# Constant matmuls in the waits of TensorE, a third weight tile split during the first gather, one more job of weight prefetch, and more ticks per step of later routing

## The chip, the cores and the metric

One core of a Trainium2 chip runs the whole program as one launch. The metric is device microseconds of one execution; the number compared is the median of several executions.

## The reference

Three stages in a row, all float32:

```
attn:  4 batches x 8 heads, 512 local + 32 global queries, head size 64
       local: |i-j| <= 32 window plus the 32 global keys; global: all 544 keys
x = attn output as [2304 tokens, 512]
moe:   logits = x @ w_gate                       # 8 experts
       for (token, e) by falling logit: take it if the token is free and e has < 288 tokens
       h = relu(x[mask] @ w1[e]); out[mask] = h @ w2[e]        # 512 -> 1024 -> 512
moe2:  out = (silu(x @ w_gate2) * (x @ w_val)) @ w_out         # 512 -> 1536 -> 512
```

The greedy assignment fills one expert after another: each routing phase finds which expert fills next and which 288 tokens it gets.

## The kernel before

**Stages.** `attention` runs 40 units (n = 0 to 39, plus 3 to drain) of scores, softmax, transposes and products. Between them it runs steps of `Convert`, which loads the second layer's float64 weights as pairs of words (`cv_raw`, 512 KB each), takes a magnitude on ACT (L116), builds float32 words on DVE (L122 to L124) into `cv_f` and stores them to a scratch `wd` (L128). A job is loaded `LD` jobs ahead of its magnitude, in `RAWB` buffers of `cv_raw`; `cv_f` has `FB` = 4 buffers. All these loads and stores, those of q, k and v, and the stores of x go through SP's queue, in program order.

**The expert stage.** Tokens are handled as 4 groups of 2 experts. For each expert, `moe(k, e)` runs blocks h(0) to h(7) and y(0) to y(5), then y(6) and y(7) together; each block is 12 matmuls of 272 columns (a product is three: high by high, high by low, low by high). `group` then runs the second layer of both: 12 x 2 blocks of 24 such matmuls, and an output stage with 512-column matmuls. Weights come as tiles of 512 KB: a load into one of 4 `raw` buffers on SP's queue, a rounding copy on ACT (L979) and a residual on DVE (L980, "split") into one of 6 `wHL` buffers. `pump` splits the tile that is needed and at most one ahead of it, if that was asked for at least `LAG` = 4 ticks ago; `load` keeps up to 3 loads outstanding. An expert's tiles in order: w1 0, w1 1, w2 0, w1 2, w2 1, w1 3, w2 2, w2 3; h(0), h(1) use the first, h(2), h(3) the second, y(0), y(1) the third.

**Routing in the background.** `background` is a generator that walks the routing phases 0 to 7: `after(k-1)`, then `phase(k)`: `best`, six search steps (a compare L678 on DVE, 17 small matmuls L685, four small DVE operations from L688), the expert's number `eis` (from which the weight loads take their address), the ranks, and the token list `idx` (17 matmuls L743). Every block of `moe` and `group` ends with `tick()`, which resumes the generator if the number of ticks of its last yield is over. `hurry` sets those numbers: for phase 1, a yield of 1 costs none and a larger one 2 ticks; for later phases a yield of more than 1 costs one tick more as long as the conversion isn't finished (`s.cv.finished`). A moe has 14 ticks, a group's 24 blocks 48, its output stage 12.

**Fetching an expert's rows.** When a phase is done, `fetch(k)` issues three indirect gathers on POOL's queue (L880), yields how many routing ticks to let pass (`GW` = 6 for expert 1, `GL` = 12 later, counted in the yields' own numbers), then transposes three blocks on PE (L898), with a copy on ACT (xH, L900) and a residual on DVE (xL, L901) for each. `wait_for(k)`, at the start of `moe(k)`, resumes the generator again and again until x of expert k is there; then the blocks go into three PSUM banks without yields between them (`s.waiting`), else all through one bank.

**Order.** The program order of every engine is the order in which this code emits it; engines run their queues in order and wait on semaphores. For expert 0, before the change, `fetch` splits two weight tiles, and x(0) is transposed at the third routing yield after the gather.

Of the kernel before, what the change touches and what calls it, by code (L numbers as in the profile page):

```python
# [14 lines left out]
ALU = mybir.AluOpType  # L15
# [49 lines left out]
CV0, CV1 = 3, 6  # L65
QB = 8
PL = 2
RAWB, CB, FB, LD = 5, 3, 4, 3
NC = 30
EN = 36  # L70
UO, LW = 0, 39
# [470 lines left out]
class Router:  # L542
# [110 lines left out]
    def phase(s, n):  # L653
        nc, V, K, b = s.nc, s.nc.vector, s.K, s.bank
        last = n == E - 1
        if n:
            yield from s.best(n)
            yield TB, 0.0
        if not last:
            lo = s.gmin  # L660
            KS, NR = KN[0]
            cmp, ge = s.cmp[:, :, 0:KS], s.ge[:, 0:KS]
            V.tensor_scalar(s.d, s.hi, s.gmin, 1e-26, op0=ALU.subtract, op1=ALU.max)
            Td = s.Td[:, 0:KS * NR].rearrange("p (r k) -> p r k", k=KS)
            V.tensor_scalar(Td, s.io[0], s.d, None, op0=ALU.mult)
            def step(k):

                return Td[:, k, 1:2]
            def bound(k):

                V.tensor_scalar(s.m1, k1, KS - 1.5, 1e38, op0=ALU.is_ge, op1=ALU.mult)
                V.tensor_scalar(s.k2, k1, 1.0, None, op0=ALU.add)
                V.scalar_tensor_tensor(s.cd, s.k2, step(k), old, op0=ALU.mult, op1=ALU.add)
                V.scalar_tensor_tensor(s.hi, s.cd, s.m1, s.hi, op0=ALU.max, op1=ALU.min)
            parts = ((0, 9), (9, NCH)) if n == 0 else ((0, NCH),)
            for k in range(NR):
                for c0, c1 in parts:
                    V.scalar_tensor_tensor(cmp[:, c0:c1], Td[:, k, None, :].to_broadcast([128, c1 - c0, KS]), lo,  # L678
                                           s.v[:, c0:c1, None].to_broadcast([128, c1 - c0, KS]), op0=ALU.add, op1=ALU.is_le)
                if k:  # L680
                    bound(k - 1)
                yield TA, RF
                cnt = b[:, 0:KS]
                for c in range(NCH):
                    nc.tensor.matmul(cnt, s.ohr[:, c].rearrange("p r e -> p (r e)"), cmp[:, c, :], start=c == 0, stop=c == NCH - 1)  # L685

                k1, new = s.k1[k % 2], s.lo2[k % 2]
                V.tensor_scalar(ge, cnt, s.nd, -1.0, op0=ALU.is_ge, op1=ALU.add, accum_out=s.ke)  # L688
                V.tensor_reduce(k1, s.ke.to_broadcast([128, 32]), axis=AX.X, op=ALU.max, apply_transpose=True)
                V.scalar_tensor_tensor(new, k1, step(k), lo, op0=ALU.mult, op1=ALU.add)  # L690
                old, lo = lo, new

            V.scalar_tensor_tensor(s.ew, s.ke, k1, s.w8p, op0=ALU.is_ge, op1=ALU.mult)
            V.tensor_reduce(s.em, s.ew.to_broadcast([128, 32]), axis=AX.X, op=ALU.max, apply_transpose=True)
            bound(NR - 1)
            V.tensor_scalar(s.G, s.v, lo, None, op0=ALU.is_ge)
            V.tensor_scalar(s.A, s.v, s.hi, None, op0=ALU.is_ge)
            V.tensor_tensor(s.G, s.G, s.A, op=ALU.subtract)
        else:
            V.scalar_tensor_tensor(s.e8, s.pen, OUTV / 2, s.w8, op0=ALU.is_ge, op1=ALU.mult)  # L700
            V.tensor_reduce(s.em, s.e8, axis=AX.X, op=ALU.max)
            V.tensor_scalar(s.A, s.v, OUTV / 2, None, op0=ALU.is_ge)
            V.memset(s.G, 0.0)
        V.tensor_scalar(s.eis[n], s.em, -1.0, 8.0, op0=ALU.mult, op1=ALU.add)
        s.known = n
        yield 1, 0.0

        Mb = s.Mb.rearrange("p (u c) -> p u c", u=2)
        V.scalar_tensor_tensor(Mb[:, 0], s.v0, s.em, s.A, op0=ALU.is_equal, op1=ALU.mult)
        V.scalar_tensor_tensor(Mb[:, 1], s.v0, s.em, s.G, op0=ALU.is_equal, op1=ALU.mult)  # L710
        if n:
            V.scalar_tensor_tensor(Mb[:, 0], s.ac, s.em, Mb[:, 0], op0=ALU.is_equal, op1=ALU.add)

        V.tensor_tensor_scan(s.Pc[:, 1:1 + 2 * NCH], s.ones, s.Mb, 0.0, op0=ALU.mult, op1=ALU.add)
        yield 2, RP if n == 0 else 0.7
        p = b[:, 320:354]
        nc.tensor.matmul(p, s.tri, s.Mb, start=True, stop=False)
        nc.tensor.matmul(p, s.onesb, s.Pc[:, 0:2 * NCH], start=False, stop=True)

        V.scalar_tensor_tensor(s.M.rearrange("p u c -> p (u c)"), p, 1.0, s.Mb, op0=ALU.add, op1=ALU.mult)  # L720
        V.scalar_tensor_tensor(s.pp, s.M[:, 0], -1.0, s.M[:, 1], op0=ALU.add, op1=ALU.add)
        W = nc.gpsimd if n == 0 else V
        V.tensor_scalar(s.lo, s.pp, 127, None, op0=ALU.bitwise_and)
        if n == 0:
            V.tensor_copy(s.lob[:, 0:NCH], s.lo)
        V.tensor_tensor(s.hb, s.pp[:, None, :].to_broadcast([128, 4, NCH]), s.thr[:, :, None].to_broadcast([128, 4, NCH]), op=ALU.is_ge)
        yield 1, 0.0
        W.tensor_tensor(s.h3, s.hb[:, 0:3], s.hb[:, 1:4], op=ALU.subtract)
        W.tensor_tensor(s.rh, s.h3.rearrange("p k c -> p c k")[:, :, :, None].to_broadcast([128, NCH, 3, 2]),
                        s.rid[:, :, None, :].to_broadcast([128, NCH, 3, 2]), op=ALU.mult)  # L730
        for c0, c1 in ((0, 8), (8, NCH + 1)):
            yield 1, 0.0
            if n == 0:
                V.tensor_tensor(s.ol[:, :, c0:c1], s.iota2[:, :, c0:c1], s.lob[:, None, c0:c1].to_broadcast([128, 128, c1 - c0]), op=ALU.is_equal)
            else:

                x = slice(c0, min(c1, NCH))
                N = x.stop - c0
                V.tensor_tensor(s.olc[:, x], s.iota[:, None, :].to_broadcast([128, N, 128]), s.lo[:, x, None].to_broadcast([128, N, 128]), op=ALU.is_equal)
        yield TQ, 0.0  # L740
        q = b[:, 384:390]
        for c in range(NCH):
            nc.tensor.matmul(q, s.olc[:, c] if n else s.ol[:, :, c], s.rh[:, c].rearrange("p k u -> p (k u)"), start=c == 0, stop=c == NCH - 1)  # L743
        q3 = q.rearrange("p (k u) -> p k u", u=2)
        V.tensor_copy(s.idxf[n], q3[:, :, 1])
        V.scalar_tensor_tensor(s.idx[n], q3[:, :, 0], 16.0, s.idxf[n], op0=ALU.mult, op1=ALU.add)
        V.tensor_copy(s.idxf[n], s.idx[n])
# [24 lines left out]
TE = CAP  # L772
OT = 4
GW, GL = 6, 12
CV2 = 0.4
LA0 = 3
MO = 1
# [3 lines left out]
class Ffn:  # L781
# [37 lines left out]
    def background(s):  # L819
# [3 lines left out]
        for k in range(E):  # L823
            for y in s.steps(k):
                yield s.hurry(k, y)
                if pend and now is None and s.moes >= pend[0] - 1:
                    now = s.fetch(pend.pop(0))
                    left = next(now)
                    yield 1, 0.0
                elif now is not None:  # L830
                    left -= y[0]
                    if left <= 0:
                        x = next(now)
                        if isinstance(x, int):
                            left = x
                        else:
                            yield x
                            yield from now
                            now = None
            if k < E:  # L840
                s.done_phase = k
            pend.append(k)
            if now is None and s.moes >= pend[0] - 1:
                now = s.fetch(pend.pop(0))
                left = next(now)
                yield 1, 0.0
# [21 lines left out]
    def hurry(s, k, y):  # L868

        if k == 1:  # L870
            return (0 if y[0] == 1 else TA, y[1])

        return (y[0] + (y[0] > 1 and k > 1 and not s.cv.finished), y[1])

    def fetch(s, k):

# [4 lines left out]
                                         in_offset=bass.IndirectOffsetOnAxis(ap=s.R.idx[k][0:n, blk:blk + 1], axis=0))  # L881
        if k == 0:

            yield 2
            for m in range(2):
                s.pump(m, 0)
                yield 1
        else:
            yield GW if k == 1 else GL
        xH = s.pool.tile([128, 4, TE], F32R, name="xH", bufs=2)  # L890
        xL = s.pool.tile([128, 4, TE], F32R, name="xL", bufs=2)
        s.xT[k] = (xH, xL)
        for blk, n in enumerate((128, 128, 16)):
# [7 lines left out]
            nc.vector.tensor_tensor(xL[:, :, sl], p, xH[:, :, sl].bitcast(F32), op=ALU.subtract)  # L901
            yield 0, 0.0
            if not s.waiting:
                yield 1, 0.0
        s.ready.add(k)

    def convert(s, n):
# [105 lines left out]
    def wait_for(s, k):  # L1013
        s.waiting = True
        while k not in s.ready:
            next(s.bgen)
            s.load()
        s.waiting = False

    def moe(s, k, e):  # L1020
# [132 lines left out]
    def run(s, ext):  # L1153
# [3 lines left out]
        for _ in s.bgen:  # L1157
            if s.R.known == 0:
                while s.nd < LA0:
                    s.dma(s.nd); s.asked[s.nd] = -1; s.nd += 1  # L1160
            if s.done_phase == 0:
                break
        s.wait_for(0)
# [55 lines left out]
```

## Time and profile before

| | us |
|---|---|
| median of 3 executions | 929.43 (929.22 to 931.23) |
| profiled execution, its own time | 931.21 |
| its span, first to last instruction | 929.4 |
| PE busy in the span | 852.3 (92%) |
| DVE busy | 595.3 (64%) |
| ACT busy | 393.8 (42%) |
| POOL busy | 110.5 (12%) |
| mean granted TensorE clock | 0.96 of full speed |

PE is TensorE, PEld its weight loads, DVE VectorE, ACT ScalarE, POOL GpSimd, SP SyncE (here a DMA queue, SPq). A line such as L980 is a line of the kernel. In a timeline row, "x12" merges twelve instructions, and the bracket at the end gives how long the engine was idle before and what released it. PEclk is the granted TensorE clock as a share of 2.4 GHz: 1.00 is that level and 0.50 is 1.2 GHz.

### The profile page before, as it was taken

The page shows a single profiled execution, that of the slowest core. Times are in us where ns is not written, and L with a number is a line of the kernel's source. Part 1 is how long each engine was busy: PE and PEld are TensorE (multiplying, and loading weights), DVE is VectorE, ACT ScalarE, POOL GpSimd, SP SyncE. Part 2 cuts the span into 40 slices and gives each one's busy share as a digit, 9 for nine tenths or more (in the row PEclk, how much of TensorE's full clock was granted, in tenths as well). Part 3 has the DMA queues.
Part 4 walks back from the last instruction along what each step waited for, and adds up shares of the span by engine and source line. Part 5 has one row for each costly group of instructions (what it writes and reads, how often), then busy time and mean ns, then how long its engine had stood idle before and what let it go on. Part 6 is the DMA issues. An engine that isn't in the chain of part 4 may idle for free.

```text
span 929.4 us, 19215 instructions
## 1 busy us (share of the span) xinstructions
PE 852.3 (92%) x7567; PEld 787.9 (85%) x7567; DVE 595.3 (64%) x1482; ACT 393.8 (42%) x823; POOL 110.5 (12%) x189
## 2 busy tenths in 40 slices
PE   6999999727779898999999899999999999999997
PEld 5887887516769897979999898899999889999985
DVE  3687786785979887847888876466454335544410
ACT  4797887502235432314443332245344234443300
POOL 5343241020000100101101000210100020000002
PEclk9999999956979899999999999999999999999999
DMA  7898898333337632234542213365322245522101
GB/s 174 219 274 240 259 266 292 118 99 108 112 95 247 198 119 75 76 113 156 182 137 82 103 62 99 114 210 162 131 92 91 91 144 174 159 69 92 46 1 56
DMA packets 109386, 128.62 MB, mean 138 GB/s; under 512 B 57392, under 2 KB 75056, under 8 KB 109296
## 3 DMA queue, kind: packets, MB, share of 16 engines
q1 hardware_dynamic: 105856, 118.35, 41.4%
q0 software_dynamic: 2896, 8.92, 2.7%
q8 instruction: 59, 0.97, 0.4%
q14 instruction: 31, 0.25, 0.1%
q10 hardware_dynamic: 544, 0.13, 0.1%
HBM read 109.02 MB, written 18.35 MB: 137 GB/s over the span
## 4 chain that ended last, share of the span: by engine, by line
PE 52%; issue 21%; DVE 17%; ACT 4%; DMA 3%; SPq 1%; POOL 1%; POOLq 0%; DVEq 0%; ACTq 0%
PE b L1009 9%; PE b L1011 9%; PE b L1010 8%; PE b L1114 4%; PE b L1115 4%; PE b L1116 4%; DVE wHL L980 3%; PE s L303 2%; DVE r_cmp L678 2%; PE tr L323 2%; DMA cv_raw<-moe_w_val 2%; PE o L334 2%; DVE b L1091 1%; ACT dH L1092 1%; PE o L339 1%
## 5 line engine op out<-in xcount | busy, mean ns | idle before, releaser
L1009 PE MATMUL b<-yH,wHL 128*128 128x272 f32 x768 | 226.5, 295 | 0.1
L1011 PE MATMUL b<-yH,wHL 128*128 128x272 f32 x768 | 222.9, 290 | 0.0
L1010 PE MATMUL b<-yL,wHL 128*128 128x272 f32 x768 | 222.3, 290 | 0.0
L980 DVE TENSOR_TENSOR wHL<-raw,wHL 128x1024 fp32r<-128x1024 f32 x136 | 163.7, 1222 | 41.0 <-ACT wHL L979 40.2
L979 ACT CAST wHL<-raw 128x1024 fp32r<-128x1024 f32 x136 | 139.2, 1047 | 77.3 <-PE b L1116 45.7
L1009 PEld LDWEIGHTS b<-yH,wHL 128*128 128x128 f32 x768 | 146.2, 190 | 5.4 <-issue 5.0
L1010 PEld LDWEIGHTS b<-yL,wHL 128*128 128x128 f32 x768 | 146.6, 191 | 0.0
L1011 PEld LDWEIGHTS b<-yH,wHL 128*128 128x128 f32 x768 | 146.2, 190 | 0.0
L1092 ACT CAST dH<-b 128x272 fp32r<-128x272 f32 x96 | 37.1, 387 | 181.9 <-DVE b L1091 178.3
L1011 PE MATMUL b<-xH,wHL 128*128 128x272 f32 x252 | 74.6, 296 | 3.5 <-DVE wHL L980 3.4
L1011 PE MATMUL b<-dH,wHL 128*128 128x272 f32 x256 | 74.7, 292 | 2.3 <-DVE wHL L980 2.3
L1009 PE MATMUL b<-xH,wHL 128*128 128x272 f32 x252 | 75.5, 300 | 1.3 <-ACT wHL L979 0.7
L1009 PE MATMUL b<-dH,wHL 128*128 128x272 f32 x256 | 75.6, 295 | 1.0 <-ACT wHL L979 1.0
L1114 PE MATMUL b<-wHL,dH 128*128 128x512 f32 x192 | 76.4, 398 | 0.0
L1115 PE MATMUL b<-wHL,dL 128*128 128x512 f32 x192 | 75.9, 395 | 0.0
L1116 PE MATMUL b<-wHL,dH 128*128 128x512 f32 x192 | 75.8, 395 | 0.0
L1010 PE MATMUL b<-dL,wHL 128*128 128x272 f32 x256 | 74.3, 290 | 0.6 <-DVE dL L1037 0.6
L1091 DVE TENSOR_TENSOR b<-b,si 128x272 f32<-128x272 f32 x96 | 42.8, 445 | 49.4 <-PE b L1011 49.4
L1010 PE MATMUL b<-xL,wHL 128*128 128x272 f32 x252 | 73.9, 293 | 0.0
L1036 ACT ACTIVATE dH<-b 128x272 fp32r<-128x272 f32 x64 | 25.5, 398 | 106.8 <-PE b L1011 102.6
L1093 DVE TENSOR_TENSOR dL<-b,dH 128x272 fp32r<-128x272 f32 x96 | 42.4, 442 | 43.6 <-ACT dH L1092 43.6
L880 POOL DMA_INDIRECT xg<-xd,r_idx x24 | 25.7, 1072 | 296.7 <-DVE r_ac L754 104.6
(237 smaller groups left out, 1612.8 us busy)
## 6 DMA issues: line engine op xcount, KB each, us to landing
raw<-wd SPq DMA_DIRECT2D x72, 512.0 KB, 3.7
raw<-moe_w SPq DMA_DIRECT2D x64, 512.0 KB, 3.7
wd<-cv_f SPq DMA_DIRECT2D x36, 256.0 KB, 6.2
cv_raw<-moe_w_gate SPq DMA_DIRECT2D x12, 512.0 KB, 6.6
cv_raw<-moe_w_val SPq DMA_DIRECT2D x12, 512.0 KB
cv_raw<-moe_w_out SPq DMA_DIRECT2D x12, 512.0 KB, 5.5
xd<-xt SPq DMA_DIRECT2D x16, 256.0 KB, 3.8
st<-k_l SPq DMA_DIRECT2D x28, 128.0 KB, 5.5
```

Source lines behind the costliest of these rows:

```text
L880: nc.gpsimd.indirect_dma_start(out=xg[0:n, blk, :], out_offset=None, in_=s.K.xd[:, :], in_offset=bass.IndirectOffsetOnAxis(ap=s.R.idx[k][0 ...
L979: nc.scalar.copy(w[:, 0], raw)
L980: nc.vector.tensor_tensor(w[:, 1], raw, w[:, 0].bitcast(F32), op=ALU.subtract)
L1009: nc.tensor.matmul(out, wH, xH, start=start, stop=False)
L1010: nc.tensor.matmul(out, wH, xL, start=False, stop=False)
L1011: nc.tensor.matmul(out, wL, xH, start=False, stop=stop)
L1091: nc.vector.tensor_tensor(b, b, si, op=ALU.mult)
L1092: nc.scalar.copy(dH[:, f, :], b)
L1093: nc.vector.tensor_tensor(dL[:, f, :], b, dH[:, f, :].bitcast(F32), op=ALU.subtract)
L1114: nc.tensor.matmul(ob[i], dh, H[:, f % 2, :], start=f == 0, stop=False)
L1115: nc.tensor.matmul(ob[i], dl, H[:, f % 2, :], start=False, stop=False)
L1116: nc.tensor.matmul(ob[i], dh, L[:, f % 2, :], start=False, stop=f == 11)
```

## The change

Seven edits: (1) `Convert` gets 7 `cv_raw` buffers and loads a job 4 jobs ahead (5 and 3 before). (2) `eis` is computed right after `em`, before the last bound. (3) In phase 0 the operation `h3` goes from POOL to DVE. (4) `fetch(0)` emits 4 constant matmuls (128 x 512, bf16) after the gathers, splits three tiles without `pump`, and emits 6 more before the transposes; later fetches emit 8 before and 14 after their yield, each only if TensorE is then in `wait_for`. (5) A fetch for k > 0 goes on at the next routing yield once `wait_for` runs. (6) `hurry` adds its tick for all of phases 2 to 7, and a fetch yields 2 ticks between blocks. (7) `wait_for(0)` calls no `load()`, and the first three loads count as asked `LAG` ticks earlier.

```diff
-RAWB, CB, FB, LD = 5, 3, 4, 3
+RAWB, CB, FB, LD = 7, 3, 4, 4
...
             V.tensor_reduce(s.em, s.ew.to_broadcast([128, 32]), axis=AX.X, op=ALU.max, apply_transpose=True)
+            V.tensor_scalar(s.eis[n], s.em, -1.0, 8.0, op0=ALU.mult, op1=ALU.add)
             bound(NR - 1)
...
-        V.tensor_scalar(s.eis[n], s.em, -1.0, 8.0, op0=ALU.mult, op1=ALU.add)
+            V.tensor_scalar(s.eis[n], s.em, -1.0, 8.0, op0=ALU.mult, op1=ALU.add)
...
-        W.tensor_tensor(s.h3, s.hb[:, 0:3], s.hb[:, 1:4], op=ALU.subtract)
+        V.tensor_tensor(s.h3, s.hb[:, 0:3], s.hb[:, 1:4], op=ALU.subtract)
...
+W0, W1, W2, W3 = 4, 6, 8, 14
...
-                    if left <= 0:
+                    if left <= 0 or s.waiting and k > 1:
...
-        return (y[0] + (y[0] > 1 and k > 1 and not s.cv.finished), y[1])
+        return (y[0] + (y[0] > 1 and k > 1), y[1])
+
+    def warm(s, n):
+        x = s.R.iota2.rearrange("p w c -> p (w c)")[:, 0:512]
+        for _ in range(n):
+            s.nc.tensor.matmul(s.B[s.hb[1]], s.K.identb, x, start=True, stop=True)
...
         if k == 0:
+            s.warm(W0)
             yield 2
-            for m in range(2):
-                s.pump(m, 0)
+            for m in range(3):
+                s.parts(m); s.np += 1
                 yield 1
+            s.warm(W1)
         else:
+            if s.waiting:
+                s.warm(W2)
             yield GW if k == 1 else GL
+            if s.waiting:
+                s.warm(W3)
...
             if not s.waiting:
-                yield 1, 0.0
+                yield 2, 0.0
...
             next(s.bgen)
-            s.load()
+            if k:
+                s.load()
...
-                    s.dma(s.nd); s.asked[s.nd] = -1; s.nd += 1
+                    s.dma(s.nd); s.asked[s.nd] = -LAG; s.nd += 1
```

## Rows read from the trace of the kernel before

**Rows 1.** Windows by stage of the expert part: length, busy time by engine, PEclk, DMA.
```profile
core 0: us, PE busy (x) PEld busy (x) DVE busy (x) ACT busy (x) POOL busy (x), PEclk, DMA share, GB/s
214.70:251.40 36.70, 32.25 (x298) 31.06 (x299) 28.36 (x93) 9.97 (x17) 0.00 (x0) 0.87 0.19 59
251.40:264.30 12.90, 4.60 (x51) 3.57 (x50) 11.51 (x41) 2.67 (x5) 2.77 (x3) 0.64 0.46 162
264.30:295.60 31.30, 29.44 (x277) 28.43 (x278) 25.53 (x71) 15.45 (x24) 0.00 (x0) 0.93 0.58 184
295.60:386.50 90.90, 81.57 (x726) 79.71 (x725) 73.14 (x204) 33.34 (x69) 5.01 (x5) 0.96 0.41 131
317.80:326.30 8.50, 5.02 (x24) 4.98 (x23) 7.15 (x29) 2.52 (x7) 3.10 (x3) 0.63 0.87 297
```

**Rows 2.** Timelines of attention, by engine: start, length, line, idle before and releaser.
```profile
74.17 0.42 SPq L110 DMA_DIRECT2D cv_raw<-moe_w_val  x1
...
78.47 0.66 ACT L116 ACTIVATE cv_a<-cv_raw 128x512 f32<-128x512 f32 x1 [4.22 <-DMA cv_raw<-moe_w_val]
...
79.80 0.43 DVE L122 TENSOR_SCALAR cv_f<-cv_raw 128x512 int32<-128x512 int32 x1 [1.28 <-DMA wd<-cv_f]
...
80.32 0.43 PE L298 MATMUL s<-mb,identb 128*128 128x320 bf16 x2 [2.32 <-ACT p L314]
...
143.67 0.43 DVE L122 TENSOR_SCALAR cv_f<-cv_raw 128x512 int32<-128x512 int32 x1 [2.32 <-DMA wd<-cv_f]
```

**Rows 3.** Timeline of PE and POOL at the first expert.
```profile
206.61 1.77 POOL L880 DMA_INDIRECT xg<-xd,r_idx  x1 [0.30 <-issue]
...
210.70 1.12 PE L898 MATMUL b<-identf,xg 128*128 128x128 f32 x4 [5.12 <-DMA raw<-moe_w]
...
214.70 2.18 PE L1032 MATMUL b<-xH,wHL 128*128 128x272 f32 x8 [0.30 <-ACT xH L900]
```

**Rows 4.** Timeline of PE and POOL at the second expert.
```profile
251.35 0.58 PE L743 MATMUL rbank<-r_rh,r_ol 128*128 128x6 bf16 x17
...
253.41 0.97 POOL L880 DMA_INDIRECT xg<-xd,r_idx  x1 [43.87 <-DVE r_ac L754]
...
257.53 2.51 PE L898 MATMUL b<-identf,xg 128*128 128x128 f32 x12 [3.30 <-DMA xg<-xd,r_idx]
...
264.29 0.60 PE L1011 MATMUL b<-xH,wHL 128*128 128x272 f32 x1 [2.19 <-DVE wHL L980]
```

**Rows 5.** Timeline of DVE during the first expert.
```profile
231.69 0.24 DVE L688 TENSOR_SCALAR_CACHE_REDUCE r_ge<-rbank,r_nd 128x32 bf16<-128x32 f32 x1
...
233.81 1.22 DVE L980 TENSOR_TENSOR wHL<-raw,wHL 128x1024 fp32r<-128x1024 f32 x1
...
243.65 0.24 DVE L688 TENSOR_SCALAR_CACHE_REDUCE r_ge<-rbank,r_nd 128x32 bf16<-128x32 f32 x1
...
246.57 0.42 DVE L1037 SCALAR_TENSOR_TENSOR dL<-b,dH 128x272 fp32r<-128x272 f32 x1
...
248.20 2.49 DVE L739 TENSOR_TENSOR r_ol<-r_iota,r_lo 128x1024 bf16<-128x1024 f32 x2
...
252.32 0.15 DVE L745 COPY r_idxf<-rbank 128x3 f32<-128x3 f32 x1
...
254.69 0.19 DVE L765 SCALAR_TENSOR_TENSOR r_cap<-r_ohe,r_cap 128x8 f32<-128x8 f32 x1
```

**Rows 6.** Timeline of PE at a 512-column stage, full clock.
```profile
387.11 0.39 PE L1114 MATMUL b<-wHL,dH 128*128 128x512 f32 x1
...
388.52 0.39 PE L1114 MATMUL b<-wHL,dH 128*128 128x512 f32 x1
```

**Rows 7.** PE's waits, 264 to 390, then 386 to the end: total, times, longest.
```profile
PE xbank L898 <- DVE xL L901: 2.7, 1, 2.7
...
PE rbank L685 <- DVE r_cmp L678: 2.6, 3, 1.2
PE xbank L898 <- DVE xL L901: 1.0, 3, 0.4
```

## The prediction

> **What bounds the kernel now.** I read the page's slices first (PE is near full in the later ones), then the windows by stage, then the timelines where PE is idle. The loss is early. The first expert takes 36.7 us, with PE's clock at 0.87 on average and DVE busy for 28.4; then come 12.9 us in which PE works for 4.6; then the second expert, 31.3 us; then the first group's blocks, 90.9 us with DVE busy for 73.1 [rows 1]. So in the first two experts TensorE waits for the router and the splits, both on DVE. The wait of 12.9 us is a chain: the second expert's ranks are turned into `idx` by L743 only after the first expert's last block (251.35), then the gathers (253.41), then the transposes (257.53), and then a split on DVE that ends the last wait at 264.29 [rows 4]. Attention is bound by PE, with two stalls; in the first ACT waits 4.22 us for a `cv_raw` load that SP had issued only at 74.17, and PE 2.32 us for ACT [rows 2].
>
> **Deeper prefetch.** A load is issued one conversion step earlier in SP's order, so the job whose load stood at 74.17 gets its place before the v loads, and ACT's 4.22 us go. But on DVE the next wait stands right beside it: L122 waits at 79.80, and again for 2.32 us at 143.67, for a store of `cv_f` to land [rows 2], and `cv_f` keeps 4 buffers. Queued behind that L122 is the maximum that the next exponential needs. At the first stall PE could start its next scores at 78.0 (80.32 less 2.32), and the unit after them still waits for DVE. Bounds: both stalls gone, each 2.32 of idle and, as an estimate, half as much again for the half-clock stretch that follows, 2 x 2.32 x 1.5 = 7.0, so -7.0; nothing gained, and one load more at the start, 0.42 of SP's queue, in the way of the q and k loads, so +0.4. I take -2.5, nearer to the small end, since two of the three waits in these rows are for stores.
>
> **Earlier `eis`, `h3` on DVE.** `eis` comes about 1 us earlier for expert 0's loads and adds nothing (one DVE operation moves along its own queue). `h3` on DVE takes the place of a POOL operation and its hand-over; I count 0.4 us earlier `idx`, hidden behind the next part's DVE work, so nothing in the sum; without that cover it would be -0.4. Leaving out `load()` in `wait_for(0)` changes little: SP's queue holds nothing else there, and the fourth load goes as soon as its buffer is free whatever its place in the program.
>
> **The first expert, by hand.** The first constants (4 + 6) stand in PE's queue in the wait of 5.12 us before the first transposes [rows 3]. A 512-column matmul passes every 0.235 us at full clock (1.41 us for six) [rows 6], 0.47 at 1.2 GHz; ten are 4.7 us, under that wait, so free. If the clock is up when the rows land, the twelve matmuls of h(0) take 12 x 0.125 = 1.5 us (0.235 x 272/512) rather than 12 x 0.25 = 3 as from 214.70 (the first eight took 2.18 [rows 3]).
>
> The larger effect is that `fetch(0)` now has a third `yield 1`. Counting yields: before, x(0) is transposed at the yield after `best`, and `wait_for(0)` returns after the first compare. Now it is transposed one yield later, and `wait_for(0)` returns with search step 0 done and the second compare emitted. From there on phase 1 is one step, two ticks, ahead: its search steps are at ticks 1, 3, 5, 7, 9 rather than up to 11, and L743 at tick 13, after h(7), rather than in `wait_for(1)`. So the gathers of expert 1 go out before y(5), y(6), y(7). Its `known` comes at tick 9 and its phase is done at 13, so `pump` splits its first three tiles before the first expert ends.
>
> When does that L743 run? DVE decides. From the end of xL (215.4; the third split and the first compare now come ahead of it) it has five search steps of 2.12 us (231.69 to 233.81), the tail 2.92 (243.65 to 246.57), ranks 1.4 (246.9 to 248.2) and lists 2.49, five splits of 1.17 (1.22, overlapping a little) and eight residuals of 0.36 (0.42, likewise) [rows 5]: 10.6 + 2.9 + 1.4 + 2.5 + 5.9 + 2.9 = 26.2. L743 ends at 242.3 (0.6 for idle bits and its own time). PE then has 36 matmuls, 4.5 us: the first expert ends at 246.8 instead of 251.35. The gathered rows are there 5.6 us after L743's end (251.93 to 257.53 [rows 4]), 247.9, all three blocks some 1.4 us later, 249.3. In between PE has the 14 constants, 14 x 0.235 = 3.3, to 250.1: they just fill the gap and hold the clock. DVE has in that time `idx` and the next `after` (252.32 to 254.88, 2.6 [rows 5]), three splits (3.5) and four residuals (1.5), to 249.9. Transposes 1.3 at full clock, last copy and residual 0.9: the second expert's first matmuls start at 252.3, with their tiles split, where the last wait of that place now ends at 264.29 [rows 4]. The 8 constants ahead of the yield are not emitted, since that fetch starts outside `wait_for`.
>
> The second expert then is PE's: 16 blocks of 1.5, 0.9 for two search steps, 0.7 for small waits: 278.0 instead of 295.6. -17.6 us. It has 4.4 us at half clock less, among others.
>
> **The first group** gets this back only in part: four search steps (8.9 us of DVE) come into it, and the next phase's ranks and the rest (5.3) and some conversion leave it. DVE has 73.1 us of work in 90.9 [rows 1], with gaps at each gate that nothing fills, so I let the difference count: +1.2.
>
> **Slower routing later.** Two ticks between blocks let xL free the one transpose bank: 2.7 and 1.0 us of PE's waits go; of the 2.6 us that PE waits for compares later [rows 7] I take 2.5 with the smaller ones beside them. -6.2. Against it, phases now take 36 ticks instead of some 26, and a fetch 7 more. Counting: phase 2's L743 at tick 49, phase 3's at 92, in the third expert (ticks 89 to 102). Expert 3's rows would be transposed at about 112, but its blocks start at 103: `wait_for(3)` finds them missing, so the fetch goes on there, with 14 constants ahead of it. PE: 3.3 + 1.3 + 0.9 + hand-overs, about 6.2, less 1.7 that the transposes cost anyway: +4.5. Queued behind those constants on PE is all of that expert. For expert 5 (blocks from tick 191, first transposes at 189) two of the three blocks are late: +1.5. Experts 2, 4, 6, 7 have 14 ticks or more in hand.
>
> **Sum.** -2.5 - 17.6 + 1.2 - 6.2 + 4.5 + 1.5 = -19.1. The profiled execution took 931.21, span 929.4 and 1.8 around it; 931.2 - 19.1 = 912.1. It is the longest of the runs shown, 1.8 above their median of 929.43; from the median the forecast is 910.3.
>
> **A rule against it.** In the first expert DVE is busy while POOL issues the gathers; a gather's issue took 0.97 us in one wait and 1.77 in the other [rows 3, 4]. The Trainium skill (SBUF — State Buffer, "A bandwidth-pool intuition that's wrong") says that such a POOL-issued transfer takes about 3.1 us instead of 0.62 while a DVE copy holds a shared port, since its descriptors can't be written. By that, three gathers would come 3 x (3.1 - 0.97) = 6.4 us later and the forecast would be about 916. The rows bear out a slowing of up to 1.8 times, no more.
>
> **Rivals.**
> - *The gathers come late or DVE falls behind* (chance 0.20). With each issue at 1.77 rather than 0.97, three are 2.4 us later [rows 3, 4]; with a third more idle time on DVE in the first expert (another 4 us) L743 comes at 246, and the constants fill a wait that is longer. Gain 19.1 - 2.4 - 4 - 1 = 11.7 or less: 915 to 924. For it: DVE then has next to no slack over 33 us.
> - *More goes* (0.12). The stall at 317.80 to 326.30, 3.5 us idle and then half clock (5.0 busy, 0.63 [rows 1]), about 5.9 us, was an in-order wait of PE for DVE's conversion words and may not recur as the phases shift; and attention may give 5 instead of 2.5. 902, down to 897. Against: DVE is as full in that group as before.
> - *The pace of later routing decides* (0.06): slower than before. If it is so slow that each of experts 2 to 7 is still to be fetched at its start, six times 6.2 replace the 6.0 counted: 910.3 + 31.2 = 941. It passes the old time from the fifth such wait on. Against: four of the six have 14 ticks.
> - *It doesn't do what it says* (0.02): x(0) later, clock not held in the waits, gathers no earlier; the half-clock stretches stay and only the small terms are left: about 929.
>
> **Numbers.** The forecast has 0.60, its own range 904 to 917. 0.2% (1.9 us) is about what a measurement of this kernel tells from no change. Faster 0.92 (forecast, the first two rivals), same 0.02, slower 0.06. Range for 8 in 10: 902 (the second rival's middle) to 921 (most of the first).
>
> **What would show it.** The L743 group before the first expert's y(5), gathers some 8 us before that expert's end; PE's idle time between the first two experts under 2 us with 14 constants in it, at PEclk 1.00; the second expert under 27 us; ACT's L116 without waits over 2 us; 14 constants again in front of expert 3 and nowhere else later. Wrong would make it: DVE too full for the earlier search steps, an L743 after 246, constants in front of more than one later expert, or an attention that takes longer because SP's queue, not the prefetch, sets its pace.

## The result, and the profile after

The changed kernel takes 907.95 us (median of 4 runs, 906.17 to 909.81), the kernel before 930.33 us on the same chip: 0.9759 of the time, 95% interval 0.9734 to 0.9785, or 22.4 us less. The forecast was 910.3, the range 902 to 921. One of the six executions of the kernel c1 below took 1375.37 us at a granted clock of 0.556; no ratio here counts it, but c1's median does (912.25 without it). The profiled execution of the changed kernel took 909.81 us, with a span of 907.4 (before: 931.21 and 929.4).

Where the time went, by stages, each from the first matmul of one to the first matmul of the next, one profiled execution each:

| stage | before, us | after, us | difference |
|---|---|---|---|
| start to the first expert's first matmul | 214.70 | 211.86 | -2.8 |
| first two experts | 80.70 | 65.79 | -14.9 |
| first group, its first two parts | 91.71 | 88.81 | -2.9 |
| everything behind that | 542.29 | 540.94 | -1.4 |

(Experts and groups are counted from 0. Later stages also exchange routing work: group 1 is 8.7 us shorter, and experts 2 to 5 and group 2 together are 10.4 longer. Only their sum is a gain or a loss. And 1.5 us of the last row need not be the change's: in the profile before, the granted clock was 0.50 from 808.06 to 811.47 us, in the last group, with PE busy throughout, and that group took 73.77 us; at clock 1.00 in the profile after it took 72.26. Six of the fourteen profiles have that drop, of kernels with the edits and without.)

The windows of the changed kernel over the first expert, the gap behind it, the second expert and the first group; after the window come its length, then busy time and instruction count of PE, PEld, DVE, ACT and POOL, then PEclk, DMA share, GB/s:

```profile
211.86:244.95 33.09, 30.26 (x302) 29.14 (x299) 29.67 (x102) 11.97 (x19) 2.72 (x3) 0.93 0.33 104
244.95:250.29 5.34, 4.57 (x29) 2.65 (x28) 4.00 (x8) 1.67 (x4) 1.15 (x1) 1.00 0.91 314
250.29:277.65 27.36, 25.82 (x226) 25.27 (x227) 23.51 (x55) 13.56 (x21) 0.00 (x0) 1.00 0.54 178
277.65:366.46 88.81, 82.25 (x747) 80.88 (x745) 68.81 (x190) 33.68 (x69) 3.34 (x4) 0.96 0.41 131
```

These answer to [rows 1], but those cut the gap where its last wait ended, at 264.30; the second expert's first matmul was at 261.28 and the first group's at 295.40. From first matmul to first matmul, 36.7, 9.9, 34.1 and 91.7 us have become 33.1, 5.3, 27.4 and 88.8. In the gap PE is busy for 4.57 of 5.34 us, at clock 1.00, and the second expert never leaves that clock. The first expert still averages 0.93.

The same place in the timeline of PE (start, duration, instruction; in brackets the idle time before it and what ended it):

```profile
240.10 0.38 PE L744 MATMUL rbank<-r_rh,r_ol 128*128 128x6 bf16 x9 [0.92 <-DVE r_ol L740]
...
244.95 3.20 PE L883 MATMUL b<-r_iota,identb 128*128 128x512 bf16 x14
247.99 1.04 PE L914 MATMUL b<-identf,xg 128*128 128x128 f32 x8
249.60 0.39 PE L914 MATMUL b<-identf,xg 16*128 16x16 f32 x4 [0.58 <-DMA xg<-xd,r_idx]
...
250.29 0.39 PE L1025 MATMUL b<-xH,wHL 128*128 128x272 f32 x1 [0.19 <-ACT xH L916]
```

L744 (formerly L743) now stands ahead of the first expert's last 36 matmuls and not behind them, as in [rows 4]; the gathers follow it at 241.62, 243.36 and 244.60, so that at 247.99 most rows are there. The 14 constants fill what is left of the wait.

In attention, the wait lists of DVE and of PE up to 182 us (engine, line, what it waited for: us in total, times, longest):

```profile
DVE cv_f L122 <- DMA wd<-cv_f: 4.1, 2, 2.3
...
PE o L412 <- DVE xt L346: 3.6, 2, 1.9
```

ACT's L116 does not appear any more as a waiter (4.22 us in [rows 2]), but DVE's L122 waits for the stores of `cv_f` as before, and PE now stands still 3.6 us for DVE in two places (1.1 before).

### The profile page after: what moved, and what is told of

Same layout as the page of the kernel before. It is cut to its first block, busy times and chain, and to the rows that moved or that the text cites. A ratio compares the mean times of both kernels' runs of the same rounds, so it can differ in the third digit from the quotient of the medians.

```text
span 907.4 us, 19300 instructions
## 1 busy us (share of the span) xinstructions
PE 853.5 (94%) x7605; PEld 786.0 (87%) x7605; DVE 595.9 (66%) x1483; ACT 394.0 (43%) x823; POOL 109.9 (12%) x188
## 4 chain that ended last, share of the span: by engine, by line
PE 59%; issue 21%; DVE 13%; ACT 3%; SPq 1%; DMA 1%; POOL 1%; POOLq 0%; DVEq 0%; ACTq 0%
PE b L1025 10%; PE b L1027 10%; PE b L1026 10%; PE b L1132 4%; PE b L1134 4%; PE b L1133 4%; PE s L303 3%; PE tr L323 2%; DVE wHL L996 2%; PE o L334 2%; PE rbank L685 1%; DVE r_cmp L678 1%; PE o L339 1%; PE tr L269 1%; PE tr L358 1%
## 5 line engine op out<-in xcount | busy, mean ns | idle before, releaser
L1025 PE MATMUL b<-xH,wHL 128*128 128x272 f32 x252 | 74.5, 296 | 1.0 <-DVE xL L917 0.8
L1027 PE MATMUL b<-xH,wHL 128*128 128x272 f32 x252 | 73.0, 290 | 0.0
```

What stands on the lines that cost most here:

```text
L1025: nc.tensor.matmul(out, wH, xH, start=start, stop=False)
L1027: nc.tensor.matmul(out, wL, xH, start=False, stop=stop)
```

## The experiments

All twelve were timed beside the kernel before. For each: the time (median), its ratio to the kernel before with the 95% interval, and from its profiled execution the first expert's first matmul ("start"), the first two experts, the first group, and the rest of the span. One profile does not settle small differences: up to the first expert, "changed", b2, b3 and c1 to c4 have the same instructions in the same order, and their starts lie between 208.59 and 216.54; "changed", b2, c2, c3 and c4 are alike in the first two experts too, and these took 65.43 to 67.90. The kernel before had medians of 932.12, 931.33 and 931.18 us beside the a, b and c runs; the ratios are taken against those, and differences in us below are a ratio's part of 930.33.

| kernel | us | ratio | start | two experts | group 0 | rest |
|---|---|---|---|---|---|---|
| before | 930.33 | 1 | 214.70 | 80.70 | 91.71 | 542.29 |
| changed | 907.95 | 0.9759 [0.9734, 0.9785] | 211.86 | 65.79 | 88.81 | 540.94 |
| a1, split alone | 925.47 | 0.9923 [0.9896, 0.9949] | 213.29 | 76.56 | 91.73 | 542.32 |
| a2, yield alone | 927.41 | 0.9959 [0.9934, 0.9985] | 214.47 | 76.29 | 92.91 | 541.43 |
| a3, split and yield | 921.53 | 0.9885 [0.9860, 0.9909] | 215.79 | 70.71 | 91.36 | 542.94 |
| a4, prefetch alone | 927.27 | 0.9948 [0.9925, 0.9970] | 209.16 | 81.39 | 93.44 | 541.91 |
| b1, no constants | 907.97 | 0.9747 [0.9717, 0.9776] | 211.91 | 68.45 | 87.47 | 538.37 |
| b2, constants for the second expert only | 909.05 | 0.9759 [0.9731, 0.9786] | 211.93 | 65.43 | 88.78 | 539.96 |
| b3, old pace | 920.59 | 0.9888 [0.9854, 0.9921] | 210.39 | 71.21 | 92.09 | 543.41 |
| b4, 16 for 6 constants | 908.62 | 0.9743 [0.9716, 0.9771] | 209.34 | 67.80 | 87.53 | 542.43 |
| c1, no early start | 912.47 | 0.9815 [0.9787, 0.9844] | 212.38 | 70.91 | 88.20 | 539.01 |
| c2, old hurry | 916.36 | 0.9844 [0.9813, 0.9875] | 211.18 | 66.13 | 94.50 | 542.79 |
| c3, one tick between blocks | 915.01 | 0.9846 [0.9816, 0.9876] | 208.59 | 67.90 | 90.73 | 542.58 |
| c4, gather lag 4 | 905.75 | 0.9745 [0.9715, 0.9775] | 216.54 | 67.29 | 87.86 | 537.81 |

### One part alone, put into the kernel before

**a1, the third split without the yield.**

```
             for m in range(3):
                 s.parts(m); s.np += 1
-                yield 1
+                if m < 2:
+                    yield 1
```

> The kernel before with the third tile split during the first gather, but without the routing yield that the change puts behind that split: TensorE's order stays that of the kernel before, L743 of the second expert still behind the first expert's last block. My theory (the gain comes from the routing that runs one step ahead): only the first expert's own waits for a split go (0.99 and 2.29 us and the half-clock blocks behind them), and DVE, which gates the ranks, takes most of it back: 926 to 929. Rival, the early split is what helps: 915 to 920. Rival, the constants make the gain: 929 to 931.

It gained 0.77%, 7.2 us, more than I had given it and less than the early split's theory did, and by its profile (from the first expert's start to the end 710.6 us, 714.7 before) some 4. Its PE timeline at the end of the first expert:

```profile
245.27 0.58 PE L743 MATMUL rbank<-r_rh,r_ol 128*128 128x6 bf16 x17
...
251.92 2.50 PE L899 MATMUL b<-identf,xg 128*128 128x128 f32 x12 [3.77 <-DMA xg<-xd,r_idx]
```

L743 is still behind the last block, and from its start to the second expert's first matmul it is 10.4 us (9.9 before). What went is inside the first expert, 32.0 us up to L743 for 36.7: the waits for `wHL`, which the next kernel still shows.

**a2, the yield without the split.** One more `yield 1` behind the two `pump(m, 0)` of the kernel before.

> The kernel before with two splits in the first gather as it has, and one more routing yield behind them. L743 of the second expert goes ahead of the first expert's last three blocks. My theory: most of the 12.9 us wait between the first two experts goes, the first expert's wait for its third split stays: 918 to 922. Rival, early split: 928 to 931. Rival, constants: 927 to 931.

It gained 0.41%, 3.8 us, less than half of what I expected, by its profile 4. Its PE timeline in the first expert:

```profile
222.10 0.39 PE L1010 MATMUL b<-dH,wHL 128*128 128x272 f32 x1 [0.99 <-ACT wHL L980]
...
224.90 0.60 PE L1012 MATMUL b<-dH,wHL 128*128 128x272 f32 x1 [2.28 <-DVE wHL L981]
...
246.36 0.36 PE L743 MATMUL rbank<-r_rh,r_ol 128*128 128x6 bf16 x8 [0.57 <-DVE r_ol L739]
...
254.81 1.23 PE L899 MATMUL b<-identf,xg 128*128 128x128 f32 x8 [2.14 <-DVE yL L1060]
257.71 0.58 PE L899 MATMUL b<-identf,xg 16*128 16x16 f32 x4 [1.67 <-DMA xg<-xd,r_idx]
260.00 0.62 PE L685 MATMUL rbank<-r_cmp,r_ohr 128*128 128x32 bf16 x17 [1.71 <-DVE r_cmp L678]
```

The order is as I had counted it, L743 ahead of the last blocks, but three waits of 2.14, 1.67 and 1.71 us stand in the gap, the last for a compare of the next phase.

**a3, both.** `for m in range(3): s.parts(m); s.np += 1; yield 1` in the kernel before.

> Both of the former: third split during the first gather and the yield behind it, no constants, old prefetch, old pace of routing. My theory: 914 to 917 (of the 17.6 us counted for the first two experts some 2 go to the clock that nothing holds in the gap). Rival, early split: as the split alone. Rival, constants: 927 to 931.

921.5: they add up (7.2 + 3.8 = 11.0 against 10.7), and the first two experts come down by 10.0 us. But half of the whole gain is still missing, more than I could put down to prefetch and constants.

**a4, the prefetch.** `RAWB, CB, FB, LD = 7, 3, 4, 4` in the kernel before.

> The kernel before with the deeper prefetch of the conversion alone (7 raw buffers, loads 4 steps ahead). My theory: attention ends 2.5 us earlier and all of it reaches the end: 927.8. Rival, hidden, since the stages behind wait for routing on DVE anyway: 929.5 to 931. Rival, both stalls go: 923 to 925.

-4.8 us, interval -7.0 to -2.8. Over all profiles the first expert starts at 214.6 on average without it (4 kernels, 213.29 to 215.79) and at 211.3 with it (10 kernels, 208.59 to 216.54): 3.2 us, though nine of the ten also have edits (2), (3), (4) and (7), and the spread is wide. Alone, by its time, it reaches the end.

### One part taken out of the changed kernel

**b1, no constants** (`W0, W1, W2, W3 = 0, 0, 0, 0`).

> The changed kernel without any of its constant matmuls. My theory: the first ten did nothing (the granted clock was 0.50 in the first expert's first matmuls with them), the 14 in the gap ahead of the second expert held the clock (without them some 30 matmuls at half clock, +3), the 14 ahead of the fourth expert (number 3) cost 3.2: 907 to 910. Rival, the constants make the gain: over 918.

No measurable difference. Its PE timeline at the gap, and its windows there:

```profile
246.62 1.29 PE L914 MATMUL b<-identf,xg 128*128 128x128 f32 x8 [1.80 <-DVE yL L1077]
249.83 0.58 PE L914 MATMUL b<-identf,xg 16*128 16x16 f32 x4 [1.92 <-DMA xg<-xd,r_idx]
...
250.71 0.60 PE L1025 MATMUL b<-xH,wHL 128*128 128x272 f32 x1 [0.18 <-ACT xH L916]
```
```profile
250.00:252.00 2.00, 1.82 (x10) 1.69 (x10) 1.17 (x7) 0.21 (x1) 0.00 (x0) 0.50 0.81 314
252.00:256.00 4.00, 4.00 (x20) 4.00 (x19) 0.57 (x2) 0.40 (x1) 0.00 (x0) 0.50 0.02 6
```

Without the 14 constants the second expert starts at clock 0.50, and the first two experts take 68.45 instead of 65.79 us. That is what these constants do, 2.7 us: 0.6 in the gap and 2.3 in the second expert (29.65 for 27.36), while the first experts agree within 0.2. The other 14, ahead of expert 3, take the same back: experts 2 and 3 last 55.0 us without them and 57.5 with them.

**b2, constants for the second expert alone** (`if s.waiting and k == 1: s.warm(W3)`).

> The changed kernel without the 14 constants ahead of the fourth expert (number 3); its rows were gathered some 5 us before. My theory: their 3.2 us go: 904 to 905.5. Rival, they stand in a wait (DVE or the gather ends it): 907 to 908.5.

By its stages as I expected (65.4 and 55.0 us), in the time not to be seen: 0.9759, interval 0.9731 to 0.9786. Its profile lost 1.5 us in the last group to a lower clock, as five other kernels did there, the one before among them.

**b4, more constants behind the third split** (`W1` from 6 to 16).

> The changed kernel with 16 instead of 6 constants behind the third split. They reach to the landing of the first expert's last rows, where TensorE now waits 1.26 and 2.24 us. My theory: the clock is then up for the first expert's first 12 matmuls (1.5 us) and some transposes: 905.5 to 907. Rival, DVE sets the pace there, and nothing comes of it: 907.5 to 908.5. Rival, they delay the transposes: over 909.

No difference that can be measured. Its PE timeline and windows ahead of the first expert:

```profile
200.26 4.51 PE L883 MATMUL b<-r_iota,identb 128*128 128x512 bf16 x16
...
207.09 1.00 PE L914 MATMUL b<-identf,xg 128*128 128x128 f32 x8 [1.89 <-DMA xg<-xd,r_idx]
208.88 0.62 PE L685 MATMUL rbank<-r_cmp,r_ohr 128*128 128x32 bf16 x17 [0.79 <-DVE r_cmp L678]
209.34 2.16 PE L1050 MATMUL b<-xH,wHL 128*128 128x272 f32 x8
```
```profile
204.61:209.34 4.73, 2.06 (x31) 1.65 (x29) 4.56 (x10) 1.29 (x3) 0.00 (x0) 0.96 0.86 278
209.34:212.21 2.87, 2.87 (x19) 2.75 (x15) 2.69 (x12) 0.00 (x0) 0.00 (x0) 0.50 0.34 129
```

The clock is up while there is little to do and down again when the work comes: behind idle times of 1.89 and 0.79 us the first expert's eight matmuls take 2.16 us at 0.50, no better than with 6 constants or with none [rows 3]. The same run shows the constants of the gap hold the clock less well: there are 14 here too, but the last gathered rows came later.

```profile
241.94 3.19 PE L883 MATMUL b<-r_iota,identb 128*128 128x512 bf16 x14
...
247.72 0.39 PE L914 MATMUL b<-identf,xg 16*128 16x16 f32 x4 [1.71 <-DMA xg<-xd,r_idx]
```
```profile
248.41:277.14 28.73, 27.21 (x226) 26.80 (x227) 23.35 (x54) 13.59 (x21) 0.00 (x0) 0.94 0.49 160
```

Behind 1.71 us of idle time, where the changed kernel had 0.58, the second expert averages clock 0.94 and takes 28.73 us, not 27.36. So those constants are worth 2.7 us in one execution and less in another.

**b3, the old pace of later routing**, three lines put back at once:

```
-                    if left <= 0 or s.waiting and k > 1:
+                    if left <= 0:
-        return (y[0] + (y[0] > 1 and k > 1), y[1])
+        return (y[0] + (y[0] > 1 and k > 1 and not s.cv.finished), y[1])
-                yield 2, 0.0
+                yield 1, 0.0
```

> The changed kernel with the old pace of later routing (no additional tick once the conversion is done, one tick between blocks of a gather, no early start of a missing gather in a wait). My theory: the fourth and the sixth expert find their rows split (-6.0), the waits for the transpose bank and for compares come back (+6.2): 906 to 910. Rival, the slower pace is a large part of the gain: over 912. Rival, it only costs: under 904.

This is the run that overturned my account. 920.6 us: the three lines are worth 1.3% of the time, 12.0 us, where my terms for them came to 0.2. The loss shows in the profile mostly in two places: 5.4 us in the first two experts and 3.3 in the first group (2.5 behind them). Its PE timeline in the gap:

```profile
244.97 0.18 PE L768 MATMUL rbank<-r_c,r_onesb 128*128 128x8 bf16 x1
245.00 3.18 PE L883 MATMUL b<-r_iota,identb 128*128 128x512 bf16 x14
...
250.64 0.58 PE L685 MATMUL rbank<-r_cmp,r_ohr 128*128 128x32 bf16 x17 [1.23 <-DVE r_cmp L678]
```

Here `after` of the old phase (L768) goes ahead of the constants, and a compare of the new phase ahead of the second expert; in the changed kernel both come later.

### The three lines one by one, and the gather lag

**c1, no early start**: the first of the three lines alone.

> The changed kernel in which a wait for rows no longer lets the gather's transposes go ahead of the next routing phase's steps; the pace (additional tick, two ticks between blocks) stays. New theory, from the run with the whole old pace (its first two experts took 71.2 us, the changed kernel's 65.8, the same constants in both): this one condition is worth about 5 us in the second expert: 912 to 914. Rival, the prediction's (it priced that condition at nothing): 907 to 909.

912.5 us: 5.2 slower than the changed kernel by the ratios, and the first two experts take 70.9 us instead of 65.8, as with all three. This one condition is the loss there. Its PE timeline, and the windows of the gap and of the second expert's first matmuls:

```profile
250.15 0.39 PE L914 MATMUL b<-identf,xg 16*128 16x16 f32 x4 [0.86 <-DMA xg<-xd,r_idx]
...
252.35 0.58 PE L685 MATMUL rbank<-r_cmp,r_ohr 128*128 128x32 bf16 x17 [1.81 <-DVE r_cmp L678]
```
```profile
245.20:252.78 7.58, 4.83 (x46) 3.09 (x45) 7.27 (x20) 1.67 (x4) 1.14 (x1) 1.00 0.85 296
252.78:257.00 4.22, 3.68 (x21) 3.48 (x18) 2.79 (x12) 0.40 (x1) 0.00 (x0) 0.60 0.00 0
```

The rows are transposed about when they are in the changed kernel, but a compare of the next phase stands in PE's order between them and the second expert, and PE waits 1.81 us for it. The gap is 2.2 us longer than in the changed kernel; the second expert is 3.1 longer (30.5 for 27.4), with the clock at 0.60 in its first 4.2 us, where the changed kernel has 1.00, and with two search steps more in it.

**c2, the old hurry**: the second line alone.

> The changed kernel without the additional tick per routing step once the conversion is done. New theory: the waits for compares and ranks in the first and second group come back, some 5 to 7 us, and the wait in front of the fourth expert goes (-4): 909 to 914. Rival, the prediction's terms (2.5 back, 6.0 saved): 903.5 to 905.

7.9 us slower by the ratios, against the prediction's sign and beyond my new range as well. The waits of PE from 277 us to the end, of this kernel:

```profile
PE rbank L685 <- DVE r_cmp L678: 9.0, 8, 3.8
PE xbank L914 <- DVE xL L917: 1.7, 2, 1.0
```

**c3, one tick between blocks**: the third line alone.

> The changed kernel with one tick instead of two between the blocks of a later gather. The prediction's theory: the waits for the one transpose bank come back, up to 3.7 us, in the first group mostly: 909 to 911.5. Rival, they are hidden or made up elsewhere: 907 to 908.5.

915.0 us, above both ranges. The waits of PE in the same stretch, of this kernel:

```profile
PE xbank L914 <- DVE xL L917: 6.2, 4, 2.4
PE rbank L685 <- DVE r_cmp L678: 1.7, 3, 0.8
```

And the changed kernel's:

```profile
PE rbank L685 <- DVE r_cmp L678: 2.0, 3, 0.8
PE xbank L914 <- DVE xL L917: 1.3, 2, 0.9
```

Each line removes its own wait: the hurry 7.0 us of waits for compares, the second tick 4.9 us of waits for the transpose bank. c3 is 8.1 us slower by the ratios, but its profile, of the fastest of its five executions (911.56 us), shows only 5.7 from the first expert's start on, of which 2.1 lie in the first two experts, where the line does nothing (last section). The intervals of c2 and c3 are 3 us to either side, and singly they add to more than together (b3 less c1: 6.8, some 4 to either side). How much of the gain is whose is not settled to better than that.

**c4, a shorter gather lag** (`GL` from 12 to 4).

> The changed kernel with 4 instead of 12 ticks between a later gather and its transposes, so that the fourth expert's rows are split before it begins and no constants are issued there. My theory: the 3.2 us of constants and the transposes' hand-overs in front of it (0.8 and more) go, and the sixth expert's blocks are in time too: 902.5 to 904.5. Rival, the transposes now wait for their rows or for DVE, in TensorE's order: 907 to 911.

The median is 905.75, the ratio 0.9745 [0.9715, 0.9775]: no difference from the changed kernel that these runs can show. The stage did what was expected, experts 2 and 3 take 54.1 instead of 57.5 us and there are no constants there. The profiled execution, the slowest of its five (911.28), had its first expert only at 216.54, with the same instructions up to there. I do not call it a better kernel.

## Why the prediction was right, and where it was not

**The number** was right within 2.4 us (the gain 22.4 us for 19.1), but not by its own terms: the first two experts gave less than theirs, the later routing and the first group much more. That these errors partly cancel is luck.

**The first two experts (-17.6; measured -14.9).** The chain was as predicted, within 0.7 us at each point. L744 ends at 240.5, forecast 242.3 less the 2.5 of attention, 239.8; the first expert ends at 244.95, forecast 244.3; the second starts at 250.29, forecast 249.8. It fell short by 1.7 us in the second expert, 27.4 us for 25.7, and by 1.0 in the first, 33.1 for 32.1. What failed is the cause that it gave. I credited the shift to the third `yield 1`; alone it is worth 3.8 us, the split that it follows 7.2, and both 10.7 (a1 to a3). The remaining 5 need the condition `s.waiting and k > 1` in the background's loop, which my text did not price: I let the second expert begin when its rows are transposed, and by the old condition PE first waits in its order for a compare of the next phase, and then has the lower clock (c1: +5.1 us in these two experts). The run of the split alone also shows that the waits for `wHL` in the first expert were a loss of their own; in my sum they were hidden in the shift.

**The first constants.** Free, as predicted (b1), and without use: h(0) at 2.4 GHz in 1.5 us was wrong. It took 2.16 + 1.11 us at clock 0.50, behind waits of 1.26 and 2.24 us for rows that landed after the constants had ended, and more constants change nothing (b4). How much of these 1.8 us reaches the first expert's end is not shown: there PE waits for DVE (0.58 and 0.92 us for L740), and in the -17.6 that end went by DVE too. The 14 constants in the gap held the clock as predicted, worth 2.7 us (b1 and b2 by stages), though not in b4's execution; those in front of expert 3 cost about the same, and the sum of all constants is nothing measurable.

**Slower routing later (-6.2 + 4.5 + 1.5 = -0.2; measured -6.8, some 4 to either side: b3 less c1).** This was the mis-sized term. The waits were the right ones, read off [rows 7], but I counted only those the kernel before happened to show. With the routing shifted, the old pace would have met others: 8.5 us of waits for compares in b3 from 281 us on, 9.0 in c2. The costs came as predicted in place: 14 constants at 426 us in front of expert 3 and none later, two blocks of expert 5 transposed only in its own wait, at 597.57. In size they were smaller: c4, which avoids them, saves 3.4 and 0.9 us in these stages by its profile, not 6.0.

**First group (+1.2; measured -2.9).** Most of the difference is the waits of the paragraph above; with the old pace it is 92.1 (b3), close to the 91.7 before. The stall at 317.8 us did not recur, but L718 waits 3.81 us at 305.36 instead: the rival "more goes" did not come.

**Prefetch (-2.5; 3.2 by the starts, 4.8 by a4's time).** The mechanism was as described, L116 free and the store waits still there. In b3 against a3, which differ by prefetch, constants and edits (2), (3) and (7), the ratios are 0.9888 and 0.9885, so what of it reaches the end beside the other edits is open within some 4 us: a3's 10.7 and the 12.0 of the three lines already make up the whole gain. The earlier `eis`, `h3` on DVE and edit (7) were not tried by themselves.

**The rule against it.** The three gathers were issued in 1.44, 0.94 and 1.50 us, longer than before (0.86 to 0.97). The first ran into a split:

```profile
240.99 1.23 DVE L996 TENSOR_TENSOR wHL<-raw,wHL 128x1024 fp32r<-128x1024 f32 x1
```
```profile
241.62 1.44 POOL L890 DMA_INDIRECT xg<-xd,r_idx  x1 [34.74 <-DVE r_idxf L748]
243.36 0.94 POOL L890 DMA_INDIRECT xg<-xd,r_idx  x1 [0.30 <-issue]
```

Its issue ended 0.84 us after that split did; the gather at 206.61 in [rows 3] ended 0.83 us after its split (206.33 to 207.55), and those at 203.93 here and at 249.15 in a2 show 0.82 and 0.84. The second ran beside small operations of DVE. So the last rows were there 9.1 us after L744's end (240.48 to 249.60), where the forecast had 7.0; it cost PE only the 0.58 us in front of the last transposes, since the constants and the other transposes filled the rest. The Trainium skill (SBUF — State Buffer, "A bandwidth-pool intuition that's wrong") gives about 3.1 us instead of 0.62 for a POOL-issued transfer that overlaps a DVE copy, because it waits until DVE lets go of a shared port. The trace agrees with an issue that waits for DVE's end, here beside splits, and shows no port; the size does not carry over, since that figure is for a whole transfer and the prediction set it against an issue. No gather here took 3.1 us to issue, and the time by the rule, 916, did not come.

**The signs named beforehand** came but for two: L744 ahead of y(5), PE idle for 0.8 us in the gap with 14 constants in it at PEclk 1.00, L116 without waits, later constants in front of expert 3 only. The second expert took 27.4 us instead of under 27, and the first gather went out 3.3 us before the first expert's end (241.62 and 244.95), not some 8; the prediction's own sum (L743's end at 242.3, the expert's at 246.8) already left no room for 8.

## What to carry to other kernels

Where one engine serves a program in a written order, look for what stands ahead of the urgent work when a wait ends, and not only for the wait: 5 of the 15 us that the early gather brought hung on one condition, without which the next phase's compare stood in the queue ahead of the expert that the rows were for. Waits of the kernel before need not be the ones that a slower pace saves if another edit shifts the schedule (2.6 us of waits for compares were counted, 8.5 to 9.0 met); price the pace on the shifted order. Here constants held the clock where PE was idle for 0.8 us between them and the work (PEclk 1.00) and not where it was idle for 2.7 (b4, ahead of the first expert, 0.50); where the rows were already there, 14 of them cost 2.5 us.

## What I had not expected

In one place the order of instructions does not settle the clock. Near the end of the first expert PE waits 0.58 and 0.92 us for L740 in the changed kernel and 0.57 and 0.91 us in c3, with the same instructions in the same order. In the changed kernel's execution the blocks behind it run at full clock, in c3's at 0.54 and 0.61 for some 4 us, which makes that expert about 2 us longer (35.4 instead of 33.1). Windows of the changed kernel, then of c3:

```profile
239.00:241.00 2.00, 1.08 (x22) 0.99 (x19) 1.81 (x6) 1.55 (x2) 0.00 (x0) 1.00 0.95 344
241.00:243.00 2.00, 2.00 (x18) 2.00 (x17) 1.90 (x6) 1.17 (x2) 1.38 (x1) 1.00 0.38 133
```
```profile
238.00:240.00 2.00, 2.00 (x12) 2.00 (x11) 1.88 (x6) 1.05 (x1) 1.07 (x1) 0.54 0.42 147
240.00:242.00 2.00, 2.00 (x12) 2.00 (x11) 1.86 (x9) 0.30 (x1) 1.39 (x3) 0.61 0.69 147
```

That can account for part of the spread between executions of one kernel; how much is not shown, since one execution of each was profiled. Terms of 1 to 3 us are read here from stages whose waits and clock explain them, and the times neither confirm nor deny them.
